# Feed-forward layers in fewer products: input of the first superblock loaded during the retention, three-operation word conversion, preparations and splits rescheduled

## The chip, the cores and the metric

One core of a Trainium2 chip runs the whole program. The metric is the device time of one execution in microseconds, the median of several runs. Engines are named as in the profile: PE is TensorE (PEld its weight loads), DVE is VectorE, ACT is ScalarE, POOL is GpSimd, SP is the queue that issues most transfers.

## The reference

The input is q, k and v of 4 batches, 8 heads, 768 positions and 64 features each. A retention with a decay per head is followed by two feed-forward layers on 3072 tokens of 512 features, with 2048 hidden features.

```
for t in range(S):
    state = gamma * state + k[t] outer v[t]
    y[t]  = scale * q[t] @ state
h  = x @ w_in;   x = maximum(0.01 * h, h) @ w_out            # layer 1
h2 = x @ w_in2;  y = (h2 * sigmoid(1.702 * h2)) @ w_out2     # layer 2
```

The inputs come as 64-bit floats for the weights and 32-bit floats for the rest, and the output is 32-bit.

## The kernel before, in words

**Stages.** The program has one instruction order per engine, written by hand. First comes the retention, in 24 steps of 128 positions (4 batches of 6). From step 6 on, each step also computes one hidden tile of layer 1 for the first 512 tokens (`ffn_in`, line 252: 12 matmuls). Then a plain part computes all 16 hidden tiles for tokens 512 to 767 (the same line, 192 matmuls of 256 columns). Then the first product of layer 1 on three superblocks of 768 tokens (class `First`, line 596), the second product of layer 1 on three superblocks of 1024 tokens (class `Second`, line 785), the first product of layer 2 on four superblocks (`First` again), and its second product (`Second` again).

**Seven products.** `First` and `Second` multiply 2 by 2 blocks with seven products instead of eight, from sums and differences of the blocks. For each of the seven, the right-hand operand of a superblock is a *form*: an optional sum or difference (lines 563, 565 and the subtraction in `form`), a cast of the high part on ScalarE (line 577) and a subtraction of the low part on VectorE (line 157, the helper `subtract`). All products run as three matmuls on high and low parts of 32-bit numbers, so weights are split too: a cast on ScalarE and a subtraction on VectorE (`w_steps`, `w_split`; lines 520, 160). In `First` the work goes in *pairs* (superblock, hidden index q), each of seven products of six matmuls; after each product the clock `later2` ticks once and issues what is due, then `beside` may hand out one step of a preparation.

**Preparations.** Weights come as 64-bit floats. `words_scalar` and `words_vector` (lines 178 to 188) turn the two 32-bit halves into a 32-bit float: two operations on ScalarE, four on VectorE, then an integer addition (line 197). A `Prep` does this for half a slot of 128 by 512 weights, adds three sums (`total`) and stores the result from GpSimd's queue (line 455). There are 16 for each of "1o", "2i" and "2o" (second product of layer 1, first and second of layer 2); 26 are done along the first product of layer 1 (one each `apart` ticks), 6 along its second product (`Packed`), 16 along the first product of layer 2. The weights of layer 1's first product are converted in the retention (`convert`, `round_up`, `finish`); their sums and differences, the *factors*, go to memory (line 215) and are read back (`Factors.load`, line 895), then split (lines 899 and 157).

**The order around the change.** In the retention, step s computes scores of step s + 1 on TensorE, then its own output (`a_out`), starts a conversion (`work_first`), multiplies the output (`a_store`, line 356) and stores each third step's state block with three transfers from SP's queue (`swapped`, lines 167 and 169). After that SP issues the qkv load of step s + 4 (line 280), which needs the buffer that step s has read. SP's queue is in order, so what waits there holds up what is behind it. After the retention, `first1.load(0)` loads the first superblock's input (four transfers of 384 KB, line 558), `factors[0].load` and others follow, and `early_steps` lists at which of the 16 plain tiles which form and which factor split is issued. Places in the on-chip memory are named areas that several stages use in turn; a transfer into one waits for its last reader.

At the end of layer 1's second product, `done1` loads and makes layer 2's first forms (1, 5, 2, 6) and splits the weights of slots 0, 1 and 2 (`w_split`); the slots 3 to 7 are split along the first pairs of layer 2 (`step2`, two pairs ahead).

Of the kernel before, what the change touches and what calls it, by code (L numbers as in the profile page):

```python
# [21 lines left out]
P = 128  # L22
# [20 lines left out]
HW_MIN, HW_MAX = _word(896 << 20), _word(0x47EFFE00)  # L43
# [15 lines left out]
N_P, N_S = 26, 6  # L59
# [31 lines left out]
def retention_two_ffn(ctx: ExitStack, tc: tile.TileContext, qkv, consts, small, w1i, w1o, w2i, w2o, scratch, out):  # L91
# [73 lines left out]
    def swapped(d, s):  # L165

        nc.sync.dma_start(out=d[:, 0::2], in_=s[:, 0::2])
        for r, t in halves:
            nc.sync.dma_start(out=d[r, 1::2], in_=s[t, 1::2])
# [89 lines left out]
    def retention():  # L259
# [73 lines left out]
        def a_store(s, o):  # L333
# [55 lines left out]
        for s in range(len(steps)):  # L389
# [22 lines left out]
            if s >= len(steps) - 3:  # L412
                todo[s - len(steps) + 3].load()
# [119 lines left out]
    class First:  # L533
# [15 lines left out]
        def load(self, blk):  # L549
            col, w = self.blocks[blk]  # L550
            x = self.src(col)
            by_half = len(x.shape) == 4
            self.raw = self.at["x"][0].view(self.at["x"][1], *x.shape[1:])
# [5 lines left out]

        def early_sums(self, k, e=nc.vector):  # L560
            a = self.block
            if k == 0:
                e.tensor_tensor(out=self.tmp, in0=a(1, 0), in1=a(1, 1), op=ALU.add)
            else:
                e.tensor_tensor(out=a(1, 0), in0=a(1, 0), in1=a(0, 0), op=ALU.subtract)

        def form(self, blk, i, at=(0, 2, 3), clock=None, e=nc.vector):
# [3 lines left out]
            t = self.at["f"][i][0].view(self.at["f"][i][1], 2, 2, self.blocks[blk][1])  # L571
            self.of[blk, i] = t
            x = {1: a(0, 0), 2: a(0, 1), 3: tmp, 4: a(1, 1), 5: tmp, 6: tmp, 7: a(1, 0)}[i]
            u, v = {6: (tmp, a(0, 0)), 3: (a(0, 1), tmp)}.get(i, (None, None))
            if u is not None:
                clock.at(at[0], lambda: subtract(tmp, u, v, e))
            clock.at(at[1], lambda: nc.scalar.copy(out=t[:, 0], in_=x))
# [293 lines left out]
    prep_rings = ring([(c2, 4), (c2, 8), (c2, 0)], 4, P, 2), ring(run_of(c1, 2, 4) + [(e4, 0)], 8, P)  # L871
    names = [(kind, n) for kind in ("1o", "2i", "2o") for n in range(2 * NQ)]
    todo = [Prep(*name, prep_rings) for name in names[:N_P]]
    waiting, behind = todo[3:], collections.deque()

    retention()

# [4 lines left out]
    class Factors:  # L882
# [22 lines left out]
        def weight(self, i):  # L905
# [6 lines left out]
    a_a, d_a, f_a = areas("adf", F32R)  # L912
    p_a = Area("g")
    g_at = [run_of(a4, 2, 1.5) + run_of(d4, 2, 1.5) + run_of(t, 2, 1.5, at) for t, at in ((early, 15), (e4, 0))]
    first1 = First({"x": (early, 0), "tmp": (early, 12),
                    "f": {5: (d_a, 0), 2: (d_a, 6), 1: (a_a, 0), 6: (a_a, 6), 7: (e_a, 0), 3: (e_a, 6), 4: (f_a, 0)},
                    "g": g_at[0], "p": run_of(p_a, 2, 1.5)},
                   later2, lambda col: xd0[col // S], gd1, S, B - 1, False, lambda q, i: factors[q].weight(i),
                   {"a": (0, 1), "b": (2, 3, 6), "c": (4, 5, 7)})
# [4 lines left out]
    left, apart = [3], [4]  # L924

    def beside(clock, free=True):
        left[0] -= 1 if free else 0.5
        if left[0] <= 0 and todo:
            left[0] += apart[0]
            todo.pop(0).give(clock, behind, waiting)  # L930
        if behind:
            behind.popleft()()

    for part in first1.load(0):
        part()
    factors[0].load(slice(0, 2))
    form = lambda i, *at: first1.form(0, i, at)
    early_steps = {1: lambda: factors[0].load(slice(2, 3)), 2: lambda: factors[1].load(),
                   4: lambda: (form(1, 0, 1, 2), factors[2].load()), 6: lambda: first1.early_sums(0),
                   7: lambda: (form(5, 0, 0, 1), first1.early_sums(1)), 9: lambda: form(2, 0, 0, 1),  # L940
                   10: lambda: factors[0].high(), 11: lambda: (factors[0].low(), form(6, 0, 1, 2)),
                   12: lambda: factors[1].high(), 13: lambda: (factors[1].low(), form(4, 0, 1, 2))}
# [9 lines left out]
    def step1(n):  # L952
        if n == 0:
            apart[0] = 5
            form(7, 0, 1, 2)
            form(3, 4, 5, 6)
            later2.at(3, factors[2].high)
            later2.at(4, factors[2].low)
# [6 lines left out]
        if n == 19:  # L965
            assert not todo
            second1.begin(later2, 0, NQ, 4, 24, 2)
# [42 lines left out]
    def done1(n, blk, i, q):  # L1010
# [22 lines left out]
        if m in (45, 47, 49):  # L1033
            first2.form(0, {45: 5, 47: 2, 49: 6}[m], (0, 1, 2), later, nc.vector)
# [191 lines left out]
```

## Time and profile before

| | |
|---|---|
| median of 3 runs | 1051.15 us (1049.3 to 1051.73) |
| profiled execution | 1050.06 us, span 1048.3 us |
| TensorE busy | 98% of the span, mean granted clock 0.995 |
| VectorE busy | 80% |
| ScalarE busy | 59% |
| chain that ended last | TensorE 87%, VectorE 6%, DMA 4% |

"Busy" is the time in which an instruction of the engine runs. Idle time stands in brackets at the instruction that ended it, with what released it. The granted clock is TensorE's, 1.00 being 2.4 GHz; its other level is 1.2 GHz, so that a stretch's mean lies between 0.5 and 1. Time that TensorE is busy at a low clock is lost without showing as idle.

### The profile page before, as it was taken

The numbers are of one execution on the slowest core, as the hardware profiler recorded it, in microseconds if no ns is written. First come the engines' busy times: TensorE is split into PE (matmuls) and PEld (weight loads), VectorE is DVE, ScalarE is ACT, GpSimd is POOL, SyncE is SP. The second block draws the span as 40 slices with busy tenths as digits, with TensorE's granted clock in tenths as the row PEclk, the third lists the DMA queues.
The fourth block names the chain that finished last, engine by engine and source line by source line (L and its number), as shares of the span: only waits on it lengthen the run. The fifth ranks groups of instructions, "written<-read, shape, count | busy, mean of one in ns | idle before, by whom it ended". The sixth has DMA issues, their size and how long they took to land.

```text
span 1048.3 us, 17915 instructions
## 1 busy us (share of the span) xinstructions
PE 1026.7 (98%) x6198; PEld 914.6 (87%) x6198; DVE 835.6 (80%) x1479; ACT 616.3 (59%) x1256; POOL 194.7 (19%) x336
## 2 busy tenths in 40 slices
PE   9999997999999999999998999999999999999998
PEld 6777897999999888888886999999999888888886
DVE  5998749998864899898999558676655898887986
ACT  5865546766656675555547656565557564545443
POOL 2423222434433000000000133433323000000000
PEclk9999999999999999999999999999999999999999
DMA  9999977988866945537463847768477735635624
GB/s 321 357 362 399 315 275 255 387 276 331 294 241 257 318 121 198 199 118 245 169 201 106 317 154 242 278 227 290 170 265 262 241 101 136 187 92 144 167 81 80
DMA packets 163914, 240.56 MB, mean 229 GB/s; under 512 B 59376, under 2 KB 103152, under 8 KB 161648
## 3 DMA queue, kind: packets, MB, share of 16 engines
q1 hardware_dynamic: 136992, 164.79, 49.2%
q0 software_dynamic: 19616, 69.62, 16.9%
q10 hardware_dynamic: 7216, 5.02, 1.5%
q8 instruction: 48, 0.79, 0.3%
q14 instruction: 42, 0.34, 0.1%
HBM read 145.53 MB, written 93.85 MB: 228 GB/s over the span
## 4 chain that ended last, share of the span: by engine, by line
PE 87%; DVE 6%; DMA 4%; issue 1%; ACT 0%; SPq 0%; DVEq 0%
PE psum L785 42%; PE psum L596 35%; PE psum L252 5%; DMA h<-qkv 3%; PE psum L290 2%; DMA h<-wdt 1%; PE psum L320 1%; DVE h L157 1%; PE psum L326 1%; PE psum L313 1%; DVE c L157 1%; DVE e L157 0%; DVE c L182 0%; DVE a L157 0%; DVE c L197 0%
## 5 line engine op out<-in xcount | busy, mean ns | idle before, releaser
L785 PE MATMUL psum<-c,h 128*128 128x512 f32 x1008 | 230.9, 391 | 4.6 <-DVE c L157 3.9
L785 PEld LDWEIGHTS psum<-c,h 128*128 128x128 f32 x1008 | 189.4, 188 | 45.5 <-DVE c L157 5.2
L785 PE MATMUL psum<-e,h 128*128 128x512 f32 x768 | 179.3, 389 | 0.0
L785 PEld LDWEIGHTS psum<-e,h 128*128 128x128 f32 x768 | 144.1, 188 | 29.9
L609 POOL DMA_DIRECT2D gd<-d x160 | 86.2, 541 | 425.6 <-ACT d L618 388.9
L596 PE MATMUL psum<-c,h 128*128 128x384 f32 x576 | 110.4, 335 | 0.0
L596 PE MATMUL psum<-b,h 128*128 128x384 f32 x576 | 110.0, 334 | 0.0
L596 PEld LDWEIGHTS psum<-c,h 128*128 128x128 f32 x576 | 100.6, 188 | 0.7 <-DVE d L631 0.6
L596 PEld LDWEIGHTS psum<-b,h 128*128 128x128 f32 x576 | 100.8, 188 | 0.0
L157 DVE TENSOR_TENSOR h<-h 128x256 fp32r<-128x256 f32 (+3 forms) x162 | 71.3, 483 | 34.6 <-ACT h L520 30.2
L618 ACT ACTIVATE d<-psum 128x384 f32<-128x384 f32 x96 | 47.2, 492 | 72.9 <-PE psum L596 71.7
L738 ACT CAST c<-b 128x512 fp32r<-128x512 f32 x96 | 59.4, 621 | 50.2 <-PE psum L785 28.2
L738 ACT CAST e<-a 128x512 fp32r<-128x512 f32 x77 | 47.7, 622 | 44.5 <-PE psum L785 24.8
L157 DVE TENSOR_TENSOR c<-b,c 128x512 fp32r<-128x512 f32 x96 | 65.1, 687 | 10.1 <-ACT c L738 9.2
L596 PE MATMUL psum<-f,h 128*128 128x384 f32 x336 | 68.1, 337 | 0.0
L596 PE MATMUL psum<-d,h 128*128 128x384 f32 x288 | 58.8, 339 | 4.1 <-ACT psum L669 2.9
L596 PEld LDWEIGHTS psum<-f,h 128*128 128x128 f32 x336 | 59.8, 190 | 0.6 <-DVE d L631 0.3
L596 PE MATMUL psum<-e,h 128*128 128x384 f32 x288 | 57.6, 334 | 2.6 <-DVE e L157 2.6
L157 DVE TENSOR_TENSOR e<-a,e 128x512 fp32r<-128x512 f32 x77 | 52.3, 685 | 8.6 <-ACT e L738 8.0
L596 PE MATMUL psum<-a,h 128*128 128x384 f32 x288 | 58.1, 337 | 0.0
L596 PEld LDWEIGHTS psum<-d,h 128*128 128x128 f32 x288 | 51.3, 191 | 4.7 <-ACT psum L669 3.3
L596 PEld LDWEIGHTS psum<-e,h 128*128 128x128 f32 x288 | 50.5, 188 | 2.9 <-DVE e L157 2.9
(198 smaller groups left out, 1806.0 us busy)
## 6 DMA issues: line engine op xcount, KB each, us to landing
gd<-d POOLq DMA_DIRECT2D x160, 192.0 KB, 4.3
b<-gd SPq DMA_DIRECT2D x72, 256.0 KB, 4.2
d<-gd SPq DMA_DIRECT2D x72, 256.0 KB, 4.6
h<-qkv SPq DMA_DIRECT2D x17, 1024.0 KB, 8.0
a<-gd SPq DMA_DIRECT2D x48, 256.0 KB, 4.9
c<-w1i SPq DMA_DIRECT2D x16, 512.0 KB, 7.9
c<-w1o SPq DMA_DIRECT2D x32, 256.0 KB, 5.3
e<-w2o SPq DMA_DIRECT2D x32, 256.0 KB, 4.4
```

What stands on the lines that cost most here:

```text
L157: e.tensor_tensor(out=o, in0=x, in1=y, op=ALU.subtract)
L252: nc.tensor.matmul(out=h, lhsT=w[:, a, k], rhs=x[c][:, k], start=(i == 0), stop=(i == 3 * NP - 1), skip_group_check=True)
L290: nc.tensor.matmul(out=ps[:, e, n], lhsT=kT[r, n], rhs=qT[r, n], start=True, stop=True, skip_group_check=True)
L313: nc.tensor.matmul(out=kv[r, n], lhsT=ks[:, 2 * n + e], rhs=v[:, n, r], start=(c == 0 and n == 0), stop=True, skip_group_check=True)
L320: nc.tensor.matmul(out=out(n, e), lhsT=v[:, n, r], rhs=sm[:, e, n], start=(n < 2), stop=(c == 0), skip_group_check=True)
L326: nc.tensor.matmul(out=out(n, e), lhsT=st[c % 2][r, n], rhs=q[r, n], start=False, stop=True, skip_group_check=True)
L596: nc.tensor.matmul(out=t, lhsT=w(k, a), rhs=x[:, b, k], start=(start and m == 0), stop=(m == 5), skip_group_check=True)
L609: put = lambda: nc.gpsimd.dma_start(out=self.dst[f * NQ + q][:, cols], in_=t)
L618: nc.scalar.activation(out=dst, in_=src, func=AF.Gelu_apprx_sigmoid)
L738: nc.scalar.copy(out=t[:, 0], in_=self.block_of(*item))
L785: nc.tensor.matmul(out=t[:, j], lhsT=w[:, j, a], rhs=x[:, b], start=(new and q == 0 and m == 0), stop=(q == NQ - 1 and m == 2), skip_group ...
```

## The change

Five parts, all in the order of work and in where data lies; what is computed stays the same.

- *Words.* ScalarE now scales the upper word by 2^-112 instead of taking its absolute value, VectorE clamps to both signs, shifts into the upper word's place and merges with the sign: three operations in place of four (line 182's is gone).
- *First superblock's input.* Its four loads go out in the last four steps of the retention (`beside_steps`), into four separate places (`load_apart`), with the difference of `early_sums` in a fifth; the forms come from the start of the plain part on (`early_steps`), and the first preparation starts right behind the retention (`give_first`).
- *State blocks.* `swapped` is issued behind the qkv load of the same step; the last one of all goes to GpSimd's queue.
- *Preparations.* 24 (before 26) along the first product of layer 1, one each 5 ticks in the plain part (before 4) and 6.5 after (before 5); 18 (before 16) along the first product of layer 2, one each 8 ticks (before 7), from pair 2 on (before 6).
- *Slots.* At the end of layer 1's second product only slot 0 is split; slots 1 to 7 are split in the pair ahead of their use, at fixed ticks. Form 6 of layer 2's first superblock has only its difference made there; its cast and low part come at the first ticks of layer 2, and forms 7, 3 and 4 one tick later.

The core of the diff:

```diff
-        nc.scalar.activation(out=f.bitcast(F32), in_=high.bitcast(F32), func=AF.Abs)
+        nc.scalar.activation(out=f.bitcast(F32), in_=high.bitcast(F32), func=AF.Copy, scale=2.0**-112)
...
-        lambda f, high: nc.vector.tensor_scalar(out=high, in0=high, scalar1=0x80000000, scalar2=None,
-                                                op0=ALU.bitwise_and),
-        lambda f, high: nc.vector.tensor_scalar(out=f.bitcast(F32), in0=f.bitcast(F32), scalar1=HW_MIN,
+        lambda f, high: nc.vector.tensor_scalar(out=f.bitcast(F32), in0=f.bitcast(F32), scalar1=-HW_MAX,
                                                 scalar2=HW_MAX, op0=ALU.max, op1=ALU.min),
-        lambda f, high: nc.vector.tensor_scalar(out=f, in0=f, scalar1=3, scalar2=0x40000000,
-                                                op0=ALU.logical_shift_left, op1=ALU.bitwise_xor),
-        lambda f, high: nc.vector.scalar_tensor_tensor(out=f, in0=f, scalar=0x7FFFFFFF, in1=high,
+        lambda f, high: nc.vector.tensor_scalar(out=high, in0=f, scalar1=3, scalar2=0x7FFFFFFF,
+                                                op0=ALU.logical_shift_left, op1=ALU.bitwise_and),
+        lambda f, high: nc.vector.scalar_tensor_tensor(out=f, in0=f, scalar=0x80000000, in1=high,
...
-                swapped(xd0[b][:, c // 3], a_store.x)
+                a_store.due = xd0[b][:, c // 3], a_store.x
...
+            if a_store.due:
+                swapped(*a_store.due, nc.gpsimd if s + 1 == len(steps) else nc.sync)
+                a_store.due = None
+            for step in beside_steps.get(s - len(steps), ()):
+                step()
...
+        def load_apart(self, place, difference):
+            x = self.src(self.blocks[0][0])
...
+            self.block = lambda r, c: place[r, c]
+            self.difference = difference
+            return {rc: lambda rc=rc: nc.sync.dma_start(out=place[rc], in_=x[:, rc[0], 2 * rc[1] : 2 * rc[1] + 2])
+                    for rc in place}
...
+    beside_steps = {-4: (parts1[1, 0], parts1[1, 1]), -3: (todo[0].load, parts1[0, 0]), -2: (todo[1].load,),
+                    -1: (parts1[0, 1], todo[2].load)}
...
+    early_steps = {0: lambda: (first1.early_sums(0), form(5, 0, 1, 2)),
+                   1: lambda: (factors[0].load(slice(2, 3)), first1.early_sums(1)),
+                   2: lambda: (form(2, 0, 0, 1), factors[1].load()), 3: lambda: form(4, 0, 0, 1),
+                   4: lambda: factors[2].load(), 5: lambda: form(1, 0, 0, 1), 6: lambda: factors[0].high(),
+                   7: lambda: (factors[0].low(), form(6, 0, 1, 2)), 9: lambda: factors[1].high(),
+                   10: lambda: factors[1].low(), 12: lambda: factors[2].high(), 13: lambda: factors[2].low()}
...
-            apart[0] = 5
+            apart[0] = 6.5
             form(7, 0, 1, 2)
-            form(3, 4, 5, 6)
-            later2.at(3, factors[2].high)
-            later2.at(4, factors[2].low)
+            form(3, 3, 4, 5)
...
-                later.at(3 + 2 * u, lambda u=u: w_split(u, 3, 7))
+            later.at(4, lambda: w_split(0, 3, 7))
...
+    first2.form(0, 6, (None, 0, 1))
     for k, i in enumerate(FORMS[4:]):
-        first2.form(0, i, (2 * k + 1, 2 * k + 1, 2 * k + 2))
+        first2.form(0, i, (2 * k + 2, 2 * k + 2, 2 * k + 3))
...
-        if 1 <= n <= 5:
-            behind.extend(w_steps(n + 2, 3, 7) + w_steps(n + 2, 0, 3))
+        if n <= 6:
+            for tick, piece in zip((0, 2, 3, 5) if n else range(4), w_steps(n + 1, 0, 3) + w_steps(n + 1, 3, 7)):
+                later2.at(tick, piece)
```

## Rows read from the trace of the kernel before

**Rows 1.** The page's first part: each engine's busy time.

```profile
PE 1026.7 (98%) x6198; PEld 914.6 (87%) x6198; DVE 835.6 (80%) x1479; ACT 616.3 (59%) x1256; POOL 194.7 (19%) x336
```

**Rows 2.** Busy time by stretch: window, length, PE, PEld, DVE, ACT, POOL, clock, DMA.

```profile
220.00:230.00 10.00, 8.84 (x52) 8.55 (x51) 9.73 (x19) 6.76 (x13) 3.77 (x7) 1.00 0.81 273
...
600.00:707.00 107.00, 107.00 (x617) 106.69 (x617) 73.95 (x139) 66.87 (x133) 36.03 (x67) 1.00 0.67 230
```

**Rows 3.** TensorE in order of time, start of layer 1; in brackets idle before.

```profile
135.53 23.30 PE L252 MATMUL psum<-e,h 128*128 128x256 f32 x192
...
164.03 2.29 PE L596 MATMUL psum<-d,h 128*128 128x384 f32 x6 [2.94 <-ACT psum L669]
...
175.94 1.32 PE L596 MATMUL psum<-e,h 128*128 128x384 f32 x6 [2.60 <-DVE e L157]
...
226.74 1.28 PE L596 MATMUL psum<-d,h 128*128 128x384 f32 x6 [1.16 <-DVE d L157]
```

**Rows 4.** TensorE by stretch: window, length, busy, granted clock, DMA share, GB/s.

```profile
84.30:90.00 5.70, 5.70 (x68) 0.70 1.08 397
...
164.00:168.00 4.00, 3.97 (x14) 0.57 0.53 190
...
576.60:581.00 4.40, 4.34 (x14) 0.61 0.00 0
```

**Rows 5.** The retention: a TensorE row, an SP row, two windows as in rows 4.

```profile
84.24 1.16 PE L290 MATMUL psum<-h 64*128 64x128 f32 x16 [1.91 <-DMA h<-qkv]
...
51.47 0.38 SPq L167 DMA_DIRECT2D xd<-a  x1
...
49.00:50.00 1.00, 1.00 (x13) 1.00 0.18 66
50.00:51.00 1.00, 1.00 (x28) 1.00 0.31 86
```

**Rows 6.** In order of time, layer 1 to layer 2: TensorE, then VectorE, then ScalarE.

```profile
563.44 7.13 PE L785 MATMUL psum<-c,h 128*128 128x512 f32 x30 [0.90 <-DVE c L157]
571.39 3.04 PE L785 MATMUL psum<-c,h 128*128 128x512 f32 x12 [0.82 <-DVE c L157]
576.66 2.62 PE L785 MATMUL psum<-c,h 128*128 128x512 f32 x6 [2.23 <-DVE c L157]
...
560.62 1.29 DVE L157 TENSOR_TENSOR h<-h 128x512 fp32r<-128x512 f32 x2
...
573.97 1.17 DVE L157 TENSOR_TENSOR h<-h 128x256 fp32r<-128x256 f32 x4 [1.36 <-ACT h L160]
...
579.32 1.01 ACT L823 COPY e<-psum 128x1024 f32<-128x1024 f32 x1 [3.26 <-PE psum L785]
...
582.61 0.84 ACT L577 CAST c<-a 128x768 fp32r<-128x768 f32 x1
...
586.96 1.13 ACT L520 CAST h<-h 128x512 fp32r<-128x512 f32 x2
```

**Rows 7.** The word conversion: line 182's operations; one beside GpSimd, in order of time.

```profile
L182 DVE TENSOR_SCALAR c<-c x42: 414/422/909, 26.0 to 298.9; 128x512 uint32<-128x512 uint32 x42
...
25.95 0.80 DVE L182 TENSOR_SCALAR c<-c 128x512 uint32<-128x512 uint32 x1
...
25.18 1.28 POOL L157 TENSOR_TENSOR d<-a,c 128x512 fp32r<-128x512 f32 x1 [2.51 <-ACT c L352]
```

**Rows 8.** The plain part in order of time: VectorE, then SP's factor loads.

```profile
150.03 0.96 DVE L563 TENSOR_TENSOR b<-b 128x768 f32<-128x768 f32 x1 [6.09 <-DMA b<-xd]
...
151.77 1.07 DVE L157 TENSOR_TENSOR c<-c 128x256 f32<-128x256 f32 x3
...
157.23 0.69 DVE L197 CUSTOM_DVE_ANT_0 c<-c,c 128x1024 uint16<-128x1024 uint16 x1
157.83 1.35 DVE L157 TENSOR_TENSOR h<-h 128x256 fp32r<-128x256 f32 x3
...
142.03 9.09 SPq L895 DMA_DIRECT2D h<-wdt x9
```

More of the change, by code (lines that the diff above doesn't have):

```diff
@@ L58 @@
 QT = 2 * P
-N_P, N_S = 26, 6
+N_P, N_S = 24, 6
 ORDER1 = [q + h * NQ for q in range(NQ) for h in range(2)]
@@ L564, in early_sums @@
             else:
-                e.tensor_tensor(out=a(1, 0), in0=a(1, 0), in1=a(0, 0), op=ALU.subtract)
+                e.tensor_tensor(out=self.difference or a(1, 0), in0=a(1, 0), in1=a(0, 0), op=ALU.subtract)
         def form(self, blk, i, at=(0, 2, 3), clock=None, e=nc.vector):
@@ L870, in retention_two_ffn, with beside, give_first @@
     c1 = Area("c1")
-    prep_rings = ring([(c2, 4), (c2, 8), (c2, 0)], 4, P, 2), ring(run_of(c1, 2, 4) + [(e4, 0)], 8, P)
+    totals_at = itertools.chain(([(e4, 0)] + run_of(c1, 2, 4)) * 6, itertools.cycle(run_of(c1, 2, 4)))
+    prep_rings = ring([(c2, 4), (c2, 8), (c2, 0)], 4, P, 2), (area.view(at, 8, P) for area, at in totals_at)
     names = [(kind, n) for kind in ("1o", "2i", "2o") for n in range(2 * NQ)]
     todo = [Prep(*name, prep_rings) for name in names[:N_P]]
-    waiting, behind = todo[3:], collections.deque()
+    a_a, d_a, f_a = areas("adf", F32R)
+    p_a = Area("g")
+    g_at = [run_of(a4, 2, 1.5) + run_of(d4, 2, 1.5) + run_of(t, 2, 1.5, at) for t, at in ((early, 15), (e4, 0))]
+    first1 = First({"x": (early, 0), "tmp": (early, 12),
+                    "f": {5: (d_a, 0), 2: (d_a, 6), 1: (a_a, 0), 6: (a_a, 6), 7: (e_a, 0), 3: (e_a, 6), 4: (f_a, 0)},
+                    "g": g_at[0], "p": run_of(p_a, 2, 1.5)},
+                   later2, lambda col: xd0[col // S], gd1, S, B - 1, False, lambda q, i: factors[q].weight(i),
+                   {"a": (0, 1), "b": (2, 3, 6), "c": (4, 5, 7)})
+    left, apart = [5], [5]
+    behind, waiting = collections.deque(), todo[3:]
+    def beside(clock, free=True):
+        left[0] -= 1 if free else 0.5
+        if left[0] <= 0 and todo:
+            left[0] += apart[0]
+            todo.pop(0).give(clock, behind, waiting)
+        if behind:
+            behind.popleft()()
+    h1_end = home["h1"].view(64, 2, 2, T1).bitcast(F32)
+    place = {(1, 0): h1_end[:, 0], (1, 1): h1_end[:, 1], (0, 0): e_a.view(8, 2, T1).bitcast(F32),
+             (0, 1): early.view(0, 2, T1)}
+    parts1 = first1.load_apart(place, early.view(4, 2, T1))
+    def give_first():
+        todo.pop(0).give(later2, behind, waiting)
+        behind.popleft()()
+    beside_steps = {-4: (parts1[1, 0], parts1[1, 1]), -3: (todo[0].load, parts1[0, 0]), -2: (todo[1].load,),
+                    -1: (parts1[0, 1], todo[2].load)}
     retention()
+    give_first()
     home["h2"] = Area("h2", F32R)
@@ L923, in retention_two_ffn @@
                      gd1, {"d": (6, 7), "e": (0, 1), "f": (2, 3), "h": (4, 5)})
[L924 to L935, printed above, removed]
     factors[0].load(slice(0, 2))
     form = lambda i, *at: first1.form(0, i, at)
[L938 to L942, printed above, removed]
+    early_steps = {0: lambda: (first1.early_sums(0), form(5, 0, 1, 2)),
[4 more added lines that the diff above has]
+                   10: lambda: factors[1].low(), 12: lambda: factors[2].high(), 13: lambda: factors[2].low()}
     tiles = [*range(NQ, KF), *range(NQ)]
@@ L965, in step1 @@
         if n == 19:
-            assert not todo
-            second1.begin(later2, 0, NQ, 4, 24, 2)
+            second1.begin(later2, 0, NQ, 4, 29, 2)
+        if n == 23:
+            assert not todo and not behind
     def done_p(blk, q):
@@ L1033, in done1 @@
         if m in (45, 47, 49):
-            first2.form(0, {45: 5, 47: 2, 49: 6}[m], (0, 1, 2), later, nc.vector)
+            first2.form(0, {45: 5, 47: 2, 49: 6}[m], (0,) if m == 49 else (0, 1, 2), later)
         if i == 6 and q == NQ - 1:
```

46 lines of the change are left out of this document (21 added, 25 removed).

## The prediction, and how it comes about

> **What bounds the kernel now.** I read the busy table first. TensorE is busy for 98% of the span [rows 1], so a change can win only what it takes out of TensorE's gaps, and the time that TensorE spends below its full clock after a gap. A stretch without gaps (the second of [rows 2]) gives 107.0 us / 617 = 173 ns a matmul, so a product of six matmuls is 1.04 us, and a pair of seven products 7.3 us. The second thing to read is who is late at each gap: TensorE's rows in order of time. There are three places.
>
> (1) Start of the first feed-forward layer, after the plain part of 192 short matmuls. TensorE idles 2.94 us for a ScalarE copy, 2.60 us for a VectorE subtraction and, as the second superblock's forms come in, 1.16 us for another [rows 3]. Behind the first of these it runs 4 us at a granted clock of 0.57 [rows 4]: nearly its lower level, 1.2 of 2.4 GHz, so (1 - 0.57) x 4 = 1.7 us more. Together 7.2 us, and 1.2 us at the superblock's change. VectorE is the late one: in the stretch of the 1.16 us gap it is busy 9.73 of 10 us [rows 2].
>
> (2) The middle of the retention. One gap of 1.91 us waits for a qkv load [rows 5], and then 5.7 us run at 0.70 [rows 4], another 1.7 us.
>
> (3) The change from the first layer's second product to the second layer's first: gaps of 0.90, 0.82 and 2.23 us, each ending on VectorE's low part of an operand [rows 6], then 4.4 us at 0.61 [rows 4], 1.7 us. Sum 5.65 us.
>
> So 7.2 + 1.2 + 3.6 + 5.65 = 17.7 us can be had where the change acts. Most of the rest of TensorE's idle time is the load of the first inputs and the tail, which the change leaves alone.
>
> **The change, part by part.**
>
> *Three-operation words.* Line 182 goes: 0.42 us at the median [rows 7], 64 conversions, 27 us of VectorE. ScalarE's step only changes its function, the same size, and line 184 already waited for it in order. Where VectorE is not late this is worth nothing. It counts directly ahead of the first weight split of the retention, where two conversions stand ahead of TensorE's first feed-forward matmul: 2 x 0.42 = 0.8 us. One of them shows 0.80 instead of 0.42 us while GpSimd has a 1.28 us subtraction running [rows 7]. If all of that went it would be 1.2 us; if ScalarE's step ends last, nothing. I take 0.8, since the operation behind it would inherit the rest of GpSimd's 1.28 us. The Trainium skill, "SBUF — State Buffer", section "Who interferes with whom", says that a VectorE operation in a two-port mode and a GpSimd instruction exclude each other for the whole instruction. The 0.80 us agrees; by that rule the part is worth 0.8 us, without it 1.2.
>
> *A state block's store comes behind the step's qkv load.* Now SP waits at line 167 for VectorE's last multiplication, until 51.47 us the first time [rows 5], with the next load behind it although its buffer is free. In 49 to 51 us the DMA engines are busy 0.18 and 0.31 [rows 5]: 0.82 + 0.69 = 1.5 us of transfer time lost, in a stretch that is else full. With the load ahead of the store this is filled, and later loads come 1.5 us sooner. TensorE comes 0.8 us sooner, so 1.91 - 1.5 + 0.8 = 1.2 us of gap are left. The 1.16 us gap of [rows 3] cost no clock (the granted clock stays 1.00 in its stretch [rows 2]), so I count the 1.7 us of slow clock as won. This part with the first: 0.8 + 0.7 + 1.7 = 3.2 us; ends 0 (load as late, clock as slow) and 4.4 (no gap left).
>
> *First superblock's input within the retention.* Its four loads of 384 KB go out from the fourth last step on, in places that nobody else holds then. Before, they were behind the retention, VectorE waited 6.09 us for them, and the nine factor loads behind them went out from 142.0 us on, for 9.09 us [rows 8]. The plain part lasts 23.3 us from 135.5 us [rows 3]; VectorE can now begin when it does. Its work there: two sums, five low parts and one difference, 8 x 0.96 = 7.7 us; three factor splits at 1.35, 4.1 us; three conversions and the start of a fourth, (0.42 + 0.42 + 0.69 + 0.69 + 1.07) x 3 + 0.84 = 10.7 us (the 0.69 and 1.07 from [rows 8], the operation at line 188 taken as long as that at 197). 22.5 us in 23.3, so all the forms of the first pair stand when it starts. In that pair VectorE has 4.9 us of work (2.45 rest of the fourth conversion, 0.5 an addition of half of 0.96's columns, an estimate, and 2 x 0.96 for the last forms) against 4.2 us of TensorE, but the two forms are wanted only in the next pair. Of 7.2 us I take 6.8 as won: the difference is what VectorE could be late there. Ends: 0, and 7.2. SP carries the same transfers in another order: the qkv loads have all gone out by then, and what queues behind the four loads (three loads of weights to prepare, then the factors) is wanted some microseconds into the plain part. The last state block's store goes to GpSimd's queue, where it waits for VectorE's last multiplication; behind it stand the plain part's own stores, with six tiles of cover.
>
> *Preparations spread.* 24 instead of 26 in the first layer, one each 6.5 ticks instead of 5. Per pair VectorE had 7/5 x 3.7 = 5.2 us of preparations (four operations, an addition and three subtractions, 0.42 x 3 + 0.69 x 2 + 1.07), 1.35 of factors and 2 x 0.5 of additions: 7.6 in 7.3 us, over the limit, so that the backlog never went. Now 7/6.5 x 3.3 = 3.5, and 5.9 us with the rest. The 1.2 us at the superblock's change go; ends 0 and 1.2. The two preparations more in the second layer's first product lie beside 73.95 us of VectorE work in 107 us [rows 2].
>
> *Slots' parts one pair ahead.* Splits of two of three slots, and form 6, leave the end of the second product. Up to the first gap that is 1.29 us against 0.90, up to the last 2 x 1.29 + 1.17 + 0.96 = 4.7 against 3.95 [rows 6]. All three gaps close, and the slow clock after them goes: 5.65. But the work comes back in the first pair, which lasts four products, 4.2 us. ScalarE has there the last result's copy 1.01, casts of two forms 2 x 0.84, four weight casts 2 x 1.13 [rows 6], and three evacuations of about 0.5 each (estimate from the 1.01 us for 1,024 columns): 6.4 us. In program order form 6 has its cast at 1.04 + 0.5 us, done by 2.4, then one weight cast and one weight subtraction (0.57 + 0.65), then its own low part, 0.96: 4.6 us, where TensorE wants it at 3 x 1.04 = 3.1. That is a new gap of up to 1.5 us; I take 1.2, and 1.1 for the weights' second half and the last forms, which stand behind it: 2.3 in all, ends 0 and 4.2 (the whole surplus of ScalarE and the same again of VectorE). Net 5.65 - 2.3 = 3.35.
>
> **Sum.** 3.2 + 6.8 + 1.2 + 3.35 = 14.55 us. The profiled execution took 1050.06 us, which gives 1035.5. The median of the three runs is 1.09 us above it; I add half, 1036.0.
>
> **Rivals.**
> *R1, the retention stays bound by its transfers.* For: the DMA engines are full on both sides of the hole, and TensorE arrives sooner. Against: the hole is 1.5 us. Part one is worth 0: 1036.0 + 3.2 = 1039.2. Chance 0.14.
>
> *R2, the second layer's first pairs take it all back.* For: ScalarE's 6.4 us in 4.2. Against: it can be late a little, the next pair but one has no forms. If the new gaps reach 4.2 us and bring 1.7 of slow clock, 1036.0 + 3.6 = 1039.6; chance 0.11.
>
> *R3, the store on GpSimd is late.* Forms 1 and 6 lie where the state block is read from, so ScalarE's cast of form 1, due some 9 us into the plain part, waits for that store to be read. If that is 10 us late, the evacuations stand behind it on ScalarE, five banks give 5 x 1.46 = 7.3 us of cover, and TensorE loses 2.7 us there and most of the old gaps return: the 6.8 us fall to about 0, 1042.8. Against: GpSimd's queue is empty before it. Chance 0.09. The Trainium skill, "SBUF — State Buffer", section "SBUF: two separate sides", states that VectorE's two-port operations keep GpSimd from writing descriptors; no row here shows a store of this shape on that queue, and by that rule this rival would come true.
>
> *R4, slower.* The splits now stand in each of the first seven pairs, one pair ahead of use, in front of the pair's own copies on ScalarE. If each of these pairs lost 1.65 us, and 1.7 of clock behind it, 7 x 3.35 = 23.5 us would stand for the 2.3: 1057. It turns to slower from (14.55 + 2.3) / 7 = 2.4 us a pair on. For: TensorE falls to a slow clock behind one gap of 2.23 us. Against: before, the same splits ran in such pairs, two ahead, without a gap (the 107 us of [rows 2] are of the same product). Chance 0.05.
>
> *R5, several of R1 to R3 at once*, which leaves about the old time: 0.03. That it doesn't do what it says: if the words came out as long as before, 0.8 us and some cover are lost, within R1.
>
> **Numbers.** Forecast 0.58, R1 0.14, R2 0.11, R3 0.09, R5 0.03, R4 0.05. Predicted 1036.0. The range goes from 1031.5 (all gains at their ends, 18.45 us, give 1032.1, and the lowest run shown lies under the profiled one by 0.8) to 1043 (R3 taken in). 0.2% is about what a measurement of this kernel can tell: faster by more 0.92, within 0.03, slower 0.05.
>
> **What would show it.** Right: no row of line 182's kind with its own 0.42 us beyond three operations a conversion; no TensorE gap between 158 and 180 us above 0.5 us; VectorE's first sum at the start of the plain part; a clock of 1.00 in all three places; a gap of about 1 us in the second layer's first pair. Wrong: a gap in the plain part that ends on ScalarE (R3); several gaps in pairs 1 to 6 of the second layer (R4); TensorE waiting for qkv as long as before (R1).

## The result, and the profile after

The changed kernel takes 1032.65 us (median of 4 runs, 1032.13 to 1033.47), against 1050.62 (1049.3 to 1051.73) for the kernel before beside it: a ratio of 0.983, 95% interval 0.9813 to 0.9847. That is faster, and 3.35 us below the forecast of 1036.0, inside its range. The profiled execution took 1032.69 us, its span is 1031.0.

First the page's first part of the changed kernel, beside [rows 1]:

```profile
PE 1019.7 (99%) x6197; PEld 910.1 (88%) x6198; DVE 814.7 (79%) x1411; ACT 616.3 (60%) x1252; POOL 194.3 (19%) x339
```

TensorE's busy time fell by 7.0 us with the same matmuls. A slow matmul counts as busy, and the three slow stretches of [rows 4], (1 - 0.70) x 5.7 + (1 - 0.57) x 4 + (1 - 0.61) x 4.4 = 5.1 us, are gone; they are most of it. VectorE lost 68 instructions and 20.9 us, where 27 us was taken for the words. Next TensorE in order of time, the start of layer 1 and then every row with idle time from 34 us to layer 2's second product (line 610 is line 596 of the kernel before, 799 its 785, 250 its 252):

```profile
131.06 23.30 PE L250 MATMUL psum<-e,h 128*128 128x256 f32 x192
154.20 1.21 PE L610 MATMUL psum<-a,h 128*128 128x384 f32 x6
...
330.38 14.81 PE L799 MATMUL psum<-c,h 128*128 128x512 f32 x64 [0.63 <-ACT a L634]
...
564.06 1.31 PE L610 MATMUL psum<-b,h 128*128 128x384 f32 x6 [1.09 <-DVE b L157]
567.68 0.45 PE L610 MATMUL psum<-b,h 128*128 128x384 f32 x1 [0.23 <-DVE h L157]
573.10 1.32 PE L610 MATMUL psum<-c,h 128*128 128x384 f32 x6 [0.49 <-DVE c L157]
...
613.36 0.45 PE L610 MATMUL psum<-b,h 128*128 128x384 f32 x1 [0.46 <-DVE h L157]
```

The gap of [rows 5] is gone, those of [rows 3] are gone, those of [rows 6] are gone; four small ones stand in layer 2's first product, 1.09 + 0.23 + 0.49 + 0.46 = 2.27 us, which the kernel before did not have. TensorE by stretch (columns as in rows 4, with every engine's busy time ahead of the clock) shows the clock at 1.00 in the places of [rows 4]:

```profile
84.00:90.00 6.00, 6.00 (x76) 4.82 (x76) 4.72 (x8) 1.92 (x4) 0.70 (x2) 1.00 1.01 352
164.00:168.00 4.00, 4.00 (x25) 4.00 (x24) 3.08 (x7) 1.93 (x5) 2.64 (x5) 1.00 0.71 260
559.50:563.50 4.00, 3.47 (x20) 3.15 (x18) 0.92 (x2) 3.60 (x7) 0.00 (x0) 1.00 0.51 146
```

The stages are read from the start of TensorE's first row in each. Their lengths in us (the last one to the end of the span):

| profiled run | start to first product | layer 1, first | layer 1, second | layer 2, first | layer 2, second | span |
|---|---|---|---|---|---|---|
| before | 158.67 | 185.52 | 234.89 | 234.74 | 234.48 | 1048.3 |
| changed | 154.20 | 176.18 | 229.11 | 237.25 | 234.26 | 1031.0 |
| difference | -4.5 | -9.3 | -5.8 | +2.5 | -0.2 | -17.3 |

Three lines of the SP queue and of VectorE show two of the moves: the qkv load leaves at 45.67 us ahead of the store at 49.26 (before, the store of [rows 5] was first), and VectorE's first sum stands 0.7 us into the plain part, where [rows 8] have it at 14.5 us.

```profile
45.67 0.33 SPq L278 DMA_DIRECT2D h<-qkv  x1
49.26 0.38 SPq L167 DMA_DIRECT2D xd<-a  x1
...
131.80 0.95 DVE L575 TENSOR_TENSOR b<-h 128x768 f32<-128x768 f32 x1
```

### The profile page after: what moved, and what is told of

Same layout as the page of the kernel before. It is cut to its first block, busy times and chain, and to the rows that moved or that the text cites. A ratio compares the mean times of both kernels' runs of the same rounds, so it can differ in the third digit from the quotient of the medians.

```text
span 1031.0 us, 17889 instructions
## 1 busy us (share of the span) xinstructions
PE 1019.7 (99%) x6197; PEld 910.1 (88%) x6198; DVE 814.7 (79%) x1411; ACT 616.3 (60%) x1252; POOL 194.3 (19%) x339
## 4 chain that ended last, share of the span: by engine, by line
PE 66%; issue 26%; DVE 3%; DMA 2%; POOL 2%; ACT 1%; ACTq 0%; SPq 0%; POOLq 0%; DVEq 0%
PE psum L610 34%; PE psum L799 20%; PE psum L250 7%; PE psum L288 2%; DMA h<-qkv 2%; PE psum L318 2%; POOL gd L623 2%; PE psum L311 1%; PE psum L324 1%; ACTq L1136 0%; DVE c L1128 0%; DMA gd<-d 0%; DVE c L807 0%; DVE e L157 0%; DVE b L291 0%
## 5 line engine op out<-in xcount | busy, mean ns | idle before, releaser
L645 DVE TENSOR_TENSOR psum<-psum,g 128x384 f32<-128x384 f32 x56 | 31.5, 563 | 25.0 <-PE psum L610 24.4
```

Source lines behind the costliest of these rows:

```text
L645: nc.vector.tensor_tensor(out=o, in0=x, in1=y, op=ALU.add)
```

## The experiments

Each is the changed kernel with one thing undone, or the kernel before with one thing done, unless it says otherwise. Runs of one version mostly agree within 1 to 2 us, but those of the kernel before spread over 4, so the intervals of the ratios are wider than most differences here; versions are therefore compared by their medians and, for the place, by the stage lengths of their profiled runs. The versions ran in four sets beside the kernel before, and the changed kernel itself in a fifth; the medians of the kernel before lie between 1049.95 and 1050.62 us in the five, so a difference of less than about 0.7 us between two sets tells nothing. The stage up to the first product moves by 1 to 2 us between versions with the same retention (153.81 to 156.12 us), with waits for the first inputs at 20 to 35 us; the other stages are steadier.

**The words alone, in the kernel before** (`p1_words_only`; the first two hunks of the diff above and `HW_MAX`, nothing else).

> The kernel before with the three-operation words alone. Theory A (each part of the change removes its own gap; the words are worth little by themselves): the first weight splits of the retention come 0.8 us sooner, the wait for the qkv load near 84 us stays, and at the start of layer 1, where VectorE is late, five conversions give back 5 x 0.42 = 2.1 us at most: 1 to 3 us off 1050.6. Rival B (VectorE's relief is what counts, wherever it was late): 5 us or more off, with the gaps at the start of layer 1 and at the superblock's change gone.

1045.92 us, ratio 0.9961 (0.9943 to 0.9978), 4.0 us less than the kernel before in the same runs. That is between the two expectations. The retention is 2.3 us shorter (first product at 156.34), and the 1.91 us gap of [rows 5] has become three, of 0.75, 0.32 and 0.86 us. Their sum, 1.93 us, is no shorter, but the clock behind them is at 1.00: most of the 2.3 us is slow clock that did not come. Layer 1's first product lasts 185.48 us, as before. At its start stand gaps of 2.51, 0.85 and 2.38 us, and the slow clock is behind the last of them. At the superblock's change the 1.16 us gap of [rows 3] is down to 0.30 us (at 224.37), with one of 0.33 at 209.21. So some 0.6 us less VectorE work per pair did shrink that gap, but it did not shorten the stage.

```profile
161.28 1.31 PE L594 MATMUL psum<-d,h 128*128 128x384 f32 x6 [2.51 <-ACT psum L667]
...
172.52 1.77 PE L594 MATMUL psum<-e,h 128*128 128x384 f32 x6 [2.38 <-DVE e L157]
```

**Four-operation words in the changed kernel** (`p2_four_words`):

> The changed kernel with four operations for a word again. Theory A: 0.8 us more in the retention, and little elsewhere, since the plain part has 22.5 + 4 x 0.42 = 24.2 us of VectorE work for 23.2 us then: 1 to 2.5 us over 1032.7. Rival B: the gaps at the start of layer 1 come back, 5 us or more over.

1034.06 us (ratio 0.9848, 0.9833 to 0.9862): 1.4 us more. Of that, 1.2 us are in the retention (first product at 155.38: a gap of 1.37 where the changed kernel has 0.96, one of 0.54, one of 0.66 for qkv) and 0.7 in the first product.

**Each state block's store ahead of the qkv load again** (`p3_store_first`):

```diff
-                a_store.due = xd0[b][:, c // 3], a_store.x
+                swapped(xd0[b][:, c // 3], a_store.x, nc.gpsimd if s + 1 == len(steps) else nc.sync)
```

> The changed kernel with the state block's store ahead of the qkv load again, the last store still on GpSimd's queue. Theory A: the hole in the transfers and the wait for qkv come back, with the slow clock behind it: 1.9 + 1.7 = 3.6 us over 1032.7, and the plain part starts at 134.7 instead of 131.1 us. Rival C (the load was late because VectorE held up the store, which three operations mend): under 1 us.

1033.7 us (ratio 0.9845, 0.9829 to 0.9861): 1.05 more, close to the rival's "under 1 us". The first product starts at 156.61, 2.4 us later, 1.2 of them already in front of the first feed-forward matmul. SP's queue has the store at 50.17 and the load behind it at 52.83, 7 us later than in the changed kernel; the DMA engines show the hole again (0.11 in the microsecond from 49, where the changed kernel has 0.93), and the gap at 84 us is back, without a slow clock behind it. SP and then TensorE:

```profile
50.17 0.38 SPq L167 DMA_DIRECT2D xd<-a  x1
50.60 2.13 SPq L169 DMA_DIRECT2D xd<-a  x2
52.83 1.08 SPq L278 DMA_DIRECT2D h<-qkv  x1
...
83.76 1.16 PE L288 MATMUL psum<-h 64*128 64x128 f32 x16 [1.57 <-DMA h<-qkv]
```

**The last state block's store on SP's queue** (`p4_last_on_sp`):

```diff
-                swapped(*a_store.due, nc.gpsimd if s + 1 == len(steps) else nc.sync)
+                swapped(*a_store.due)
```

> The changed kernel with the last state block's store on SP's queue, in its place behind the retention's last step. Theory A: SP waits for VectorE's last multiplication at 131.8 us, with the fourth input load, one load of weights and the first factors behind it; these come some 3 us later. The forms that need the fourth load are due 3 us into the plain part: 0 to 1.5 us over 1032.7. Rival (GpSimd's queue was the only safe place): 4 us or more over.

1034.45 us (ratio 0.985, 0.9826 to 0.9873): 1.8 more, a little above the 0 to 1.5 expected; its four runs spread over 2.7 us. The first product lasts 178.81 us instead of 176.18, with gaps of 0.90 us at 161.70 and 1.11 at 302.68. Three of the four loads of the input have gone out by then; the last one, at 133.49 us, one load of weights and the factors stand behind the store.

**The first superblock's input behind the retention, forms in the old order** (`p5_input_late`; `beside_steps` without the four `parts1`, `first1.load(0)` and `early_steps` of the kernel before):

> The changed kernel with the first superblock's input loaded behind the retention and the forms issued at the plain tiles where the kernel before issued them; words, spacing, stores and slots as in the change. Theory A: VectorE waits some 6 us for the input again and TensorE idles at the start of layer 1's first product: 4 to 7 us over 1032.7, less than the 7.2 us of the kernel before since VectorE's work is shorter. Rival B (shorter words and fewer preparations did it): under 2 us.

1032.84 us (ratio 0.9838, 0.9824 to 0.9853): within 0.2 us of the changed kernel, first product 177.05 us. Loading the input in the retention's last steps is not needed. But the input was not as late as in the kernel before: the first load left at 123.04, the other three from 130.34 us on. VectorE's first sum came at 140.59, 9.3 us into the plain part, not 14.5 (SP, then VectorE):

```profile
130.34 2.46 SPq L561 DMA_DIRECT2D b<-xd  x3
...
140.59 0.95 DVE L575 TENSOR_TENSOR b<-b 128x768 f32<-128x768 f32 x1
```

**The old order and the last store on SP's queue** (`p12_late_on_sp`): the run before this one with the edit of `p4_last_on_sp` as well, so that the loads stand behind the store as they did in the kernel before.

> The changed kernel with the first superblock's input loaded behind the retention and the old order of forms (as one run before had it, at 1032.84 us), and now the last state block's store on SP's queue as well, so that the four loads stand behind that store as they did in the kernel before. In that run the loads left SP's queue from 123.0 us on, 13 us ahead of the kernel before, since the store no longer stood in front of them, and VectorE's first sum came at 140.6 us instead of 150.0. Theory A (the input's arrival is what counts, and either change alone brings it): the loads go out behind the end of the retention again, first sum at 145 to 148 us, the old gaps at the start of the first product come back, 3 to 7 us with their slow clock, time 1036 to 1040. Rival B (the wide spacing alone gives VectorE room enough, whenever the input comes): no gap above 0.5 us there beyond the 0.9 us that the store on SP cost by itself, time 1033 to 1035.

1037.8 us (ratio 0.9889, 0.9869 to 0.9909): 5.0 us more than with that store on GpSimd's queue (4.2 by the first product, 181.21 against 177.05). SP, VectorE and TensorE in order of time:

```profile
132.13 0.37 SPq L167 DMA_DIRECT2D xd<-a  x1
132.54 1.24 SPq L169 DMA_DIRECT2D xd<-a  x2
133.88 1.44 SPq L441 DMA_DIRECT2D c<-w1o  x2
135.43 2.60 SPq L561 DMA_DIRECT2D b<-xd  x4
...
145.73 0.96 DVE L575 TENSOR_TENSOR b<-b 128x768 f32<-128x768 f32 x1 [5.06 <-DMA b<-xd]
...
159.27 0.97 PE L610 MATMUL psum<-d,h 128*128 128x384 f32 x4 [2.43 <-ACT psum L683]
```

Here the first sum stands 14.5 us into the plain part, exactly as in [rows 8], and the gap of [rows 3] is back with 2.43 us and a slow clock behind it:

```profile
159.30:163.30 4.00, 4.00 (x15) 4.00 (x16) 3.76 (x8) 2.66 (x6) 1.45 (x3) 0.62 1.05 393
```

The chain behind it on ScalarE: the cast of a form at 155.33 waits 2.29 us for VectorE, and the copy that frees a bank (line 683; a bank is a place that TensorE writes its results to) comes behind it at 158.73. So what counts is when the input arrives, and two parts of the change bring it, each without the other: a store that no longer stands ahead of the loads in SP's order does it within 0.2 us, loads issued in the retention within 1.8.

**The old spacing** (`p6_spread_back`):

```diff
-    left, apart = [5], [5]
+    left, apart = [4], [4]
-            apart[0] = 6.5
+            apart[0] = 5
```

> The changed kernel with its preparations spaced as before: one each 4 ticks in the plain part and 5 after, 24 in all. Theory A: VectorE has 7/5 x 3.3 + 2.35 = 7.0 us of work in a pair of 7.3 us and never catches up with a delay; the gap at the superblock's change comes back in part, and a little at the first pair: 0.5 to 2 us over 1032.7. Rival (the three-operation words alone bring VectorE under the limit): within 0.3 us.

1039.17 us (ratio 0.9897, 0.9879 to 0.9914): 6.5 more, which neither expectation has; first product 182.72 us, with no gap at its start. ScalarE, then TensorE, around the largest gap:

```profile
242.02 0.66 ACT L178 ACTIVATE c<-c 128x512 f32<-128x512 f32 x1 [2.52 <-DMA wd2i<-c]
252.72 0.66 ACT L178 ACTIVATE c<-c 128x512 f32<-128x512 f32 x1 [3.08 <-DMA wd2i<-c]
253.85 0.47 ACT L683 COPY psum<-psum 128x384 f32<-128x384 f32 x1
...
254.38 1.54 PE L610 MATMUL psum<-d,h 128*128 128x384 f32 x6 [2.29 <-ACT psum L683]
```

Behind that gap TensorE runs 5.6 us at 0.70, another 1.7 us. ScalarE waits for the store of an earlier preparation to have left its place. This is a side of the edit that was not meant: the change also lets the ring of result places fall from three to two for the last 6 preparations (`totals_at`, one place is wanted by something else late in the stage), which the wide spacing allows and the old one does not.

**The old spacing with the old ring of three places** (`p9_close_three`):

```diff
-    totals_at = itertools.chain(([(e4, 0)] + run_of(c1, 2, 4)) * 6, itertools.cycle(run_of(c1, 2, 4)))
-    prep_rings = ring([(c2, 4), (c2, 8), (c2, 0)], 4, P, 2), (area.view(at, 8, P) for area, at in totals_at)
+    prep_rings = ring([(c2, 4), (c2, 8), (c2, 0)], 4, P, 2), ring(run_of(c1, 2, 4) + [(e4, 0)], 8, P)
-    left, apart = [5], [5]
+    left, apart = [4], [4]
-            apart[0] = 6.5
+            apart[0] = 5
```

> The changed kernel with the old spacing of the preparations (4 and 5 ticks) and, unlike the run that only put the spacing back, with the old ring of three result places for all of them; the changed kernel's ring falls to two places for its last 6 preparations. Theory A (what the close spacing lost was turnover: in that run ScalarE waited at line 178 for the store from a result place, 2.5 and 3.1 us, with the evacuations behind it): the gap of 2.29 us near 254 us and its slow clock go, the one of 1.22 us near 200 us, which waited for a raw load, stays; first product 178 to 179 us long, time about 1034.5 to 1035.5. Rival B (close spacing overloads the engines themselves): first product stays at 182 to 183, time about 1039.

1034.99 us (ratio 0.9864, 0.9844 to 0.9884), first product 178.49 us: the gap at 254 is gone, the one at 200 stays. The spacing itself is worth 2.3 us here, and the other 4.2 of the run before were the missing place, the 1.7 us of slow clock behind its gap included. Most of what is left of it also begins with a transfer, of raw weights this time, and with the copy of line 683 behind ScalarE's wait (ScalarE, then TensorE):

```profile
198.65 0.66 ACT L178 ACTIVATE e<-c 128x512 f32<-128x512 f32 x1 [2.08 <-DMA c<-w1o]
199.78 0.47 ACT L683 COPY psum<-psum 128x384 f32<-128x384 f32 x1
...
200.30 1.32 PE L610 MATMUL psum<-d,h 128*128 128x384 f32 x6 [1.15 <-ACT psum L683]
```

From 180 to 200 us the DMA share is 1.04 there, 0.95 in the changed kernel.

**The same with the input late** (`p10_late_close_three`): the edits of `p9_close_three` and `p5_input_late` together.

> As the run before it in this call, with the first superblock's input loaded behind the retention and the old order of forms too. Theory (early input and wide spacing replace each other: each alone leaves VectorE enough room ahead of the first product): the old gaps at the start of the first product return, 2.5 and 2.4 us with about 2 us of slow clock and the gap of 0.85, so that the first product is 5 to 7 us longer than with the early input, time about 1040 to 1042. Rival (the early input is worth nothing in either case, as it was with wide spacing): within 0.5 us of the run before it, 1035 to 1036.

1036.88 us (ratio 0.9882, 0.9858 to 0.9906), first product 180.62 us: 1.9 more than with the early input, where wide spacing made it 0.2. A gap of 1.58 us at 166.50 waits for a form's low part. That lies between the two expectations: the gaps of [rows 3] do not come back in full. This run too has the last store on GpSimd's queue, which fits; the old spacing with that store on SP's was not run.

**The slots' parts as before** (`p7_slots_back`; `done1` and the ticks of forms 7, 3 and 4 of the kernel before; slots 3 to 7 stay one pair ahead, and the spacing is the changed one):

> The changed kernel with slots 1 and 2 split, and form 6 made, at the end of layer 1's second product as before; slots 3 to 7 still one pair ahead. Theory A: the three gaps and the slow clock behind them come back (5.65 us before), the gaps of 2.3 us in layer 2's first pairs go: 3.4 us over 1032.7. Rival (the end of the second product was late because of the packed preparations' fourth operation or of earlier lateness): the gaps do not come back and the kernel is 1 to 2 us faster than the change.

1035.02 us (ratio 0.9856, 0.9837 to 0.9874): 2.4 more, where 3.4 was expected. The old gaps are back, 0.90, 0.86 and 2.23 us with the slow clock behind the last, and layer 2's first pairs have none: layer 1's second product lasts 235.16 us instead of 229.11 and layer 2's first 233.80 instead of 237.25.

```profile
550.13 7.09 PE L799 MATMUL psum<-c,h 128*128 128x512 f32 x30 [0.90 <-DVE c L157]
558.09 3.04 PE L799 MATMUL psum<-c,h 128*128 128x512 f32 x12 [0.86 <-DVE c L157]
563.36 2.93 PE L799 MATMUL psum<-c,h 128*128 128x512 f32 x6 [2.23 <-DVE c L157]
```

**Form 6 finished inside layer 1's second product** (`p8_form6_end`), a new version: there VectorE has room four items after the one that makes the difference (an item is one of the seven products for one slot).

```diff
+        if m == 53:
+            first2.form(0, 6, (None, 0, 1), later)
...
-    first2.form(0, 6, (None, 0, 1))
...
-        first2.form(0, i, (2 * k + 2, 2 * k + 2, 2 * k + 3))
+        first2.form(0, i, (2 * k + 1, 2 * k + 1, 2 * k + 2))
```

> The changed kernel with form 6's cast and low part issued three items before the end of layer 1's second product, where ScalarE is idle for 3.7 us and VectorE for 5.2 us, and forms 7, 3 and 4 one tick sooner; the slots as in the change. Theory A (the first 1.09 us gap of layer 2 is form 6 queued behind a weight split): that gap goes and half of the others, 1.2 to 2 us under 1032.7. Rival (ScalarE's sum of work in the first two pairs sets the loss): the gap moves to a later product and the time stays within 0.5 us.

1030.7 us (1030.36 to 1032.07; ratio 0.9817, 0.9798 to 0.9835), by the medians 1.95 less than the changed kernel, and its slowest run lies under that kernel's fastest. Its second product is no longer (229.08 us), and layer 2's first is 234.73. One gap is left there:

```profile
568.86 0.45 PE L610 MATMUL psum<-b,h 128*128 128x384 f32 x1 [0.87 <-DVE h L157]
```

**And form 3 one tick later, on top of the version before it** (`p11_form3_later`):

```diff
-        first2.form(0, i, (2 * k + 1, 2 * k + 1, 2 * k + 2))
+        c = 2 * k + 1 + (k > 0)
+        first2.form(0, i, (c, c, c + 1))
```

> The version with form 6's cast and low part at the end of layer 1's second product, and forms 3 and 4 of layer 2's first superblock one tick later again (form 7 stays). Theory: the one gap left there, 0.87 us, waits for a weight's low part that stands on VectorE right behind form 3's difference (0.95 us); with that difference a tick later the low part goes first, the gap closes and nothing else opens: time about 0.9 us under that version's 1030.7, so 1029.5 to 1030.2. Rival: form 3's own low part is then wanted before it is there and a gap of up to 0.9 us opens one or two pairs on: 1030.5 to 1031.

1030.47 us (1029.99 to 1031.44; ratio 0.9821, 0.9801 to 0.9842): no difference from the version before it that these runs can tell, so the rival and not the theory. The gap moved: 0.49 us, now for a form's low part.

```profile
571.14 1.32 PE L610 MATMUL psum<-c,h 128*128 128x384 f32 x6 [0.49 <-DVE c L157]
```

## Why the prediction was right, and where it was not

The sign, the three places and the two signs in layer 2 were right: a first product shorter by its gaps, an end of the second product without gaps, new gaps of 2.27 us in layer 2's first pairs where 2.3 was taken. The forecast sum was 14.55 us, the spans differ by 17.3; with the half microsecond that was added for the median, that is the error of 3.35. Undone one at a time, the words, the store's order, the early loads with the last store, the spacing and the slots cost 1.4 + 1.05 + 5.15 + 2.3 + 2.4 = 12.3 us of the 18.0 between the medians; no run here divides the rest. By its terms:

*Words and the store behind the load: 3.2 taken, 4.5 measured* (the stage up to the first product, good to about 2 us). The words' 0.8 us in front of the first feed-forward matmul holds: with four operations back in the changed kernel the two waits there are 1.37 and 0.54 us instead of 0.96 and 0.19, 0.76 more. Two other parts of the step were off. The gap was to stay with 1.2 us; none stayed. With the store ahead of the load again it is 1.57, so the order alone took that much. And the 1.7 us of slow clock was credited to the store, while with the store ahead of the load and a gap of 1.57 us the clock stayed at 1.00, and with the words alone, the store still ahead, it stayed at 1.00 too. Undone one at a time the two cost 1.4 and 1.05 us by the medians, 1.2 and 2.4 by the start of the first product.

*First superblock's input, 6.8 us, and preparations spread, 1.2: together 8.0 taken, 9.3 measured, and the cause of the first was the wrong one.* The step that failed is the one that counted the loads' place in the program, "Its four loads of 384 KB go out from the fourth last step on", as what wins 6.8 us, and the store on GpSimd's queue only as a risk. Undone alone the early loads cost 0.2 us; undone with that store back on SP's queue, 5.2 (1037.8 against 1032.65). So, with the changed spacing, the early loads win only where the store would otherwise hold them (with the old spacing they are worth 1.9 us besides): what had made the input late was that store, ahead of it in an in-order queue. [rows 8] show the wait's end, and the row that would have told is SP's, of the kernel before, just ahead of the factor loads of [rows 8]:

```profile
136.38 0.37 SPq L167 DMA_DIRECT2D xd<-a  x1
136.79 1.24 SPq L169 DMA_DIRECT2D xd<-a  x2
138.14 1.36 SPq L439 DMA_DIRECT2D c<-w1o  x2
139.61 2.32 SPq L558 DMA_DIRECT2D b<-xd  x4
```

The four loads wait for a store that waits for VectorE's last multiplication (135.66 us in that trace). With the store elsewhere and the changed spacing they need not move: a first sum 9.3 us into the plain part is early enough, one at 14.5 is not. Nor was the sum of VectorE's work in the plain part (22.5 in 23.3 us), which was to show that all forms stand in time, what decides.

*Spread, 1.2 us, from VectorE's 7.6 us of work per pair in 7.3:* the size is 2.3 with three result places, more than its upper end, and VectorE's total is not the whole reason. The words alone brought that total under the limit by the same sum (7.0); the 1.16 us gap, which ended on VectorE, then fell to 0.30, but the stage stayed at 185.48 us. In the two runs with the old spacing and the early input the largest gaps end on ScalarE's copy (1.22 and 2.29 us, 1.15 with three places; 0.25 us in each ends on VectorE): ScalarE, in order, waits for a preparation's transfer with that copy behind it. The stretch's VectorE is now at 7.46 of 10 us.

*Slots' parts: 3.35 net taken, 2.4 measured by undoing them.* The gain is 6.05 us (5.65 taken), the stage lengths of layer 2's first product give 3.45 back (2.3 taken). Of these, 2.27 are idle time in brackets, and the rest stands in the same four places, read from start to start:

```profile
560.73 2.24 PE L610 MATMUL psum<-b,h 128*128 128x384 f32 x12
564.06 1.31 PE L610 MATMUL psum<-b,h 128*128 128x384 f32 x6 [1.09 <-DVE b L157]
565.21 1.20 PE L610 MATMUL psum<-f,h 128*128 128x384 f32 x6
...
577.55 2.24 PE L610 MATMUL psum<-b,h 128*128 128x384 f32 x12
579.63 2.24 PE L610 MATMUL psum<-c,h 128*128 128x384 f32 x12
```

Where TensorE runs on, twelve matmuls have a row of 2.24 us and the next row starts after 2.08: recorded ends reach 0.16 us past the next start. Idle time in brackets counts from such an end, so it is 0.16 us too short; and the six matmuls behind the gap take 1.15 us to the next start, not 1.04. The first place cost 564.06 - 560.73 - 2.08 + 0.11 = 1.36 us, the four 1.36 + 0.51 + 0.88 + 0.73 = 3.48. The prediction summed brackets in layer 1 too. By starts, the three gaps of [rows 3] lost 3.10 + 2.77 + 1.33 = 7.20 us where the brackets have 6.70; with the slow clock and about 0.1 behind each of the other two that is 9.1 us of the 9.3 measured there. TensorE's rows just ahead of them in the kernel before (six matmuls are 1.04 us):

```profile
159.89 1.21 PE L596 MATMUL psum<-d,h 128*128 128x384 f32 x6
...
172.13 1.20 PE L596 MATMUL psum<-a,h 128*128 128x384 f32 x6
...
224.37 1.21 PE L596 MATMUL psum<-e,h 128*128 128x384 f32 x6
```

The place and its order were right: the first new gap waits for form 6's low part, 1.09 us where up to 1.5 was worked out and 1.2 taken, and moving that form's work ahead of the stage took 1.95 us off.

*Rivals.* R1 did not come (no gap waits for qkv between 34 and 154 us); R2 came in part: the pairs gave back 3.45 us, more than the 2.3 taken and less than its 4.2, with no slow clock; R4 did not: no later gap is over 0.49 us. R3 did not: the store on GpSimd's queue went at once,

```profile
132.19 0.73 POOL L167 DMA_DIRECT2D xd<-a  x1 [11.46 <-DVE a L354]
132.91 1.23 POOL L169 DMA_DIRECT2D xd<-a  x2
```

and ScalarE's cast of form 1 started at 140.28 without a wait on that store. In these 1.95 us VectorE was busy for 1.92. The Trainium skill, "SBUF — State Buffer", section "Who interferes with whom", speaks of transfers issued by GpSimd that starve for ports beside VectorE. These rows show at most 0.36 us of it: the two transfers of line 169 took 1.23 us to issue, 1.24 on SP's queue, and the first 0.73 against 0.37.

## What to carry to other kernels

Before a transfer is moved up in the program, look at what stands ahead of it on its queue: one store that waits for a last result held four loads back, and giving the store another queue did the work of issuing the loads earlier. When two parts of a change could each do the same, undoing one shows nothing: undo both, and see that the cause came back (here, the time of VectorE's first sum) before the time is read. When a spacing is put back for a test, put back what it allowed too: a ring one place shorter looked like 4.2 us of spacing. And read what a gap cost from start to start: the idle time in brackets was 0.16 us short at each of the seven read so here.

## What the runs showed of the hardware that was not expected

**The clock's price of a gap isn't fixed.** Gaps of nearly one length went with either level behind them. 2.51 us at 161.28 (the words alone) left the clock at 1.00, and 2.38 us at 172.52 in the same trace had 0.69 over 5.5 us; 2.43 us at 159.27 (old order, last store on SP) had 0.62 over the next 4 us. The words alone:

```profile
161.30:165.30 4.00, 4.00 (x23) 4.00 (x24) 3.90 (x7) 4.00 (x9) 1.69 (x4) 1.00 0.58 201
```

```profile
172.50:178.00 5.50, 5.48 (x22) 5.48 (x23) 3.50 (x8) 1.27 (x3) 1.99 (x4) 0.69 0.87 285
```

The end of layer 1's second product has nearly the same three gaps in three traces (0.90, then 0.82 to 0.86, then 2.21 to 2.23 us): the clock behind the last was 0.61 [rows 4] and 0.64 with the slots' parts put back, and 1.00 with the words alone. The last two, in stretches of 4.4 us, the slots' parts put back first, then the words alone:

```profile
563.40:567.80 4.40, 4.40 (x15) 3.82 (x16) 1.38 (x6) 1.06 (x2) 0.00 (x0) 0.64 0.00 0
```

```profile
573.30:577.70 4.40, 3.44 (x18) 3.17 (x19) 2.38 (x8) 1.83 (x4) 0.00 (x0) 1.00 0.00 0
```

(In the second the window holds the last 0.96 us of the gap too.) Nor is it fixed for one kernel: of the four runs with the slots' parts put back two have a mean clock of 0.998 and take 1035.47 and 1035.81 us, two have 1.000 and take 1034.34 and 1034.57. So 1.7 us per gap is not a price that can be counted on, and of the 4.0 us of the words alone neither the part behind the retention (2.1 us in layer 1's second product and layer 2's first, by the profiled runs) nor the 1.7 us of slow clock missing in the retention need be the words'.

**Who issues a transfer counted by what the issuer waits for.** The two versions that differ in the queue of three stores alone are 5.0 us apart (1037.8 and 1032.84; the first product 4.2). The Trainium skill, "DMA: Bandwidth & Descriptors", section "Issuing engines are not separate DMA queues", says that issuing from several engines saves only the time that it takes to issue. The rows agree that this time is small (0.37 + 1.24 us for the three), and show that the wait of an in-order issuer comes on top.
